# Five opening slots of an attention and MLP kernel with another order of work, other memsets, and one bank pool

## The chip, the cores and the metric

The kernel runs on one core of one Trainium2 chip. The metric is the device time of one execution in microseconds (us). The engines are TensorE (PE, with its weight loads shown as PEld), VectorE (DVE), ScalarE (ACT), GpSimd (POOL) and SyncE (SP). SP and POOL also issue DMAs from their queues. The inputs are drawn with a fixed seed.

## The reference

Attention with a forget gate for 8 batches of 8 heads, 576 positions, head size 64, and an MLP behind it:

```python
scores = scale * np.matmul(q, k.transpose(0, 1, 3, 2))
log_f = np.log(np.clip(f, 0.0001, 1.0))
cum = np.cumsum(log_f, axis=-1)
decay = cum[:, :, :, None] - cum[:, :, None, :]
scores = np.where(causal, -1000000000.0, scores + decay)
attn = softmax(scores)                       # over the last axis, with 1e-09 added to the sum
x = (attn @ v) in rows of 8 * 64             # 4608 rows of 512
h = x @ w_in                                 # 512 -> 2048
out = (h - np.tanh(h)) @ w_out               # 2048 -> 512
```

## The kernel before

The attention works on pairs of heads: 8 batches of 4 pairs, `pairs[p]`. A slot p holds the scores of pair p and the values of pair p - 1, so that PE does not wait for the exponentials of the pair in hand. In all but the first five slots, steps of the MLP stand between the attention's pieces. All engines follow the order in which the program emits the instructions (`tc.manual_schedule`), so each engine's queue is the order of the calls in the code. An instruction that waits holds up all that stands behind it on its engine.

**Loads.** q, k, v and the weights come by DMAs that POOL issues, and are cast to 16 bits on the way. `load_qk` brings some heads of q or k in rows of positions (`qn`, `kn`), `load_v_head`, `load_v_block` and `load_v_rest` bring v (`vn`), `load_win` a quarter of the first weight (512 of 2048 columns, which are four of the 16 tiles `ft`), `load_wout` a half of the second. Those of batches 0 and 1 and of the weights are emitted in one run before the slots. SP issues the loads of f, small rows (`const_rows`, `load_aug`), transposes from batch 1 on, and the output.

**Preparation.** VectorE clears constants and pads by memsets, clamps f, and after ACT's logarithm does the running sum (`tensor_tensor_scan`) and splits it into two 16-bit rows `chi` and `clo` (in `cc`). These are added to the scores either as extra rows of `QT`/`KT` or, for the first head, by extra matmuls (`direct` in `scores`) with `pick` as selector. `pick[:, 2:3]`, which the second head needs for tile 4 alone, is written in `pads()`.

**Pieces of a slot.** The lists `FIRST[p]` spell slots 0 to 4:

- a number: that many matmuls on constants (`spin`).
- `q`n, `k`n: `trans` for pair p + n. PE turns the head pair's q or k by six transposes into a bank from `t_bank`, and VectorE copies the bank into `QT` or `KT` in two instructions (ACT does it for the first q).
- `s`i: `scores` of tile i alone, and `g`i: of a group of tiles, (0, 1), (2, 4), (5, 6) or (3). Tiles 0 to 2 are the first head's, 4 to 6 the second's, 3 the last key block of both. ACT then takes the exponential of the bank or of both banks (L358). Tile 3 uses a bank of `t_bank` in slots 0 to 3.
- `va`, `vb`: `values` of the pair before, first and second head, 15 matmuls each, into one pair of banks `av` that exists once. After `vb` VectorE forms the reciprocal sums `rs` and divides, `xn` (L385 to L387).
- `y`, `x`: `turn` of the pair two before or one before. PE transposes `xn`, VectorE copies it into `XR`, the input of the MLP.
- `p`, `r`, `c`: `pads()`, `later_rows()`, and rows of constants.
- `h`, `m`: the first MLP matmuls of `mlp1` without their last quarter, and one step of the list `mlp`.

`t_bank` gives in slots 0 to 3 two banks in turn, `t2` and `tr`, afterwards `tr` alone. In slot 0 single tiles of scores go to four banks (`ps_one`), in slots 1 to 3 pairs of banks come from a pool of two (`ps_two`), which takes over the same memory. From slot 4 on there are three banks for the MLP and two for scores.

From slot 5 on `att_items` gives the order, with `trans` of the next pair behind given tiles, and the MLP steps are spread between the items. Each unit u of 512 rows runs 16 steps `mlp1`, one for each tile `ft` in the order `turns`: four matmuls, ACT's tanh, and VectorE's sum (`gt`). Where a pair of tiles and its partner are done, `sums` adds them for the second product, which follows in 14 steps (`product`, a scheme with seven instead of eight block products). Sums of the weight's blocks (`wsum`) stand at steps 14 to 23 of the first unit.

Of the kernel before, what the change touches and what calls it, by code (L numbers as in the profile page):

```python
# [14 lines left out]
PITCH = 640  # L15
VW = 66
SHIFT = 5.0
FAR = 3
BIG = 32768.0


@with_exitstack
def kernel(
# [63 lines left out]
    def load_qk(dst, src, b, h0, h1):  # L87
        nc.gpsimd.dma_start(
            out=dst[b % 2][:, h0:h1, :, :].rearrange("p h n d -> p (h n) d"),
            in_=src[b, h0:h1, :, :].rearrange("h s d -> (h s) d").rearrange("(m p) d -> p m d", p=S // NT6))  # L90
# [51 lines left out]
    def load_aug(b, h0=0):  # L142
# [3 lines left out]
        nc.sync.dma_start(out=KT[i][D + 1:D + 2, h0:H, 0:S], in_=cc[NH + b * H + h0:NH + b * H + H, :])  # L146

    nc.vector.memset(id16, 0.0)
    nc.vector.memset(ones16, 1.0)
    nc.gpsimd.affine_select(out=id16, in_=id16, compare_op=ALU.not_equal,  # L150
                            fill=1.0, base=0, pattern=[[-1, P]], channel_multiplier=1)
    load_qk(qn, q, 0, 2, 4)
    load_qk(kn, k, 0, 2, 4)
    nc.vector.memset(minus16, -1.0)
    const_rows(0, 1, H)
    nc.vector.memset(pick, 0.0)
    nc.vector.memset(pick[0:1, 0:1], -1.0)
# [1 line left out]
    nc.vector.memset(pick[0:1, 1:2], 1.0)  # L159
    nc.vector.memset(cqs[NH:P, :], 0.0)  # L160
    nc.vector.memset(KT[0][D:D + 3, 0, :], 0.0)
    nc.vector.tensor_scalar(out=lf, in0=lf, scalar1=0.0001, scalar2=1.0,
                            op0=ALU.max, op1=ALU.min)
    nc.vector.memset(neg16, 0.0)
    nc.vector.memset(tri16, 0.0)
    nc.vector.memset(QT[0][D:D + 3, 0, :], 0.0)
    load_qk(qn, q, 0, 4, 6)
    load_qk(kn, k, 0, 4, 6)
    nc.gpsimd.affine_select(out=neg16, in_=neg16, compare_op=ALU.not_equal,
# [16 lines left out]
    load_v_head(0, 1)  # L186
    load_v_rest(0)
    load_qk(qn, q, 0, 6, H)
    for n in range(NJ - 1):
        load_v_block(0, n, 2, H)  # L190
    load_qk(kn, k, 0, 6, H)

    def pads():
        nc.vector.scalar_tensor_tensor(out=pick[:, 2:3], in0=id16[:, 1:2], scalar=-1.0, in1=id16[:, NH + 1:NH + 2],
                                       op0=ALU.mult, op1=ALU.subtract)
        for e in EL:
            nc.vector.memset(e, 0.0)
        nc.vector.memset(KT[0][0:D, :, S:PITCH], 0.0)
        nc.vector.memset(KT[0][D:D + 3, 1:H, S:PITCH], 0.0)
        nc.vector.memset(vn[0][D:P, NJ - 1, :, :], 0.0)  # L200
        nc.vector.memset(vn[0][:, :, :, D:VW], 1.0)

    def later_rows():
        nc.vector.memset(KT[1][:, :, S:PITCH], 0.0)
        nc.vector.memset(vn[1][D:P, NJ - 1, :, :], 0.0)
        nc.vector.memset(vn[1][:, :, :, D:VW], 1.0)
        const_rows(1, 0, H)
        load_aug(1)

# [9 lines left out]
    for h0, h1, then in ((0, 2, (0, 2)), (2, 4, ("v", 1)), (4, 6, (3,)), (6, H, ())):  # L219
        load_qk(qn, q, 1, h0, h1)  # L220
        load_qk(kn, k, 1, h0, h1)
        for i in then:
            if i == "v":
                load_v(1)
            else:
                load_win(i * QW, (i + 1) * QW)
# [90 lines left out]
    def scores(b, c, tis, how):  # L317
        n2 = len(tis)
        if "t" in POOLS and tis[0] == LAST:
            banks = t_bank().rearrange("p (o w) -> p o w", o=1)  # L320
        else:
            banks = POOLS["s"].tile([P, 2 if how == "group" else 1, UW], FP32, tag="sc", name="ps")
        if tis[0] == LAST:
            eb = EL[(b * NPAIR + c) % 3].rearrange("p (o w) -> p o w", o=1)
        else:
            g, o = PLACE[tis[0]]
            if b == 0:
                if o == 0:
                    EB[(b, c, g)] = gtp.tile([P, 2, UW], FP16, tag="gt", name="e2")
                eb = EB[(b, c, g)][:, o:o + n2, :]  # L330
            else:
                eb = aex.tile([P, 1, UW], FP16, tag="e", name="e")
        for i, ti in enumerate(tis):
            ps, e = banks[:, i, :], eb[:, i, :]
            for a, j, i0, n, col in TILES[ti]:
                h = 2 * c + a
                edge = min(P, n) if how != "late" and i0 == j * P else 0
                direct = b == 0 and (h == 0 or h == 1 and ti == 4)
                minus, plus = (pick[:, 0:1], pick[:, 1:2]) if h == 0 else (pick[:, 2:3], id16[:, 1:2])
                kn_ = min(P, S - j * P) if direct else P  # L340
                rows = D if direct and h else D + 3
                nc.tensor.matmul(out=ps[:, col:col + n], lhsT=KT[b % 2][0:rows, h, j * P:(j + 1) * P],  # L342
                                 rhs=QT[b % 2][0:rows, h, i0:i0 + n], start=True, stop=not (edge or direct))
                if direct:
                    nc.tensor.matmul(out=ps[0:kn_, col:col + n], lhsT=cc[:, j * P:j * P + kn_],
                                     rhs=minus.to_broadcast([P, n]), start=False, stop=False)
                    nc.tensor.matmul(out=ps[:, col:col + n], lhsT=plus.to_broadcast([P, P]),
                                     rhs=cqs[:, i0:i0 + n], start=False, stop=not edge)
                if edge:
                    nc.tensor.matmul(out=ps[:, col:col + edge], lhsT=neg16, rhs=tri16[:, 0:edge],  # L350
                                     start=False, stop=True)
                for ib in range(j, NJ):
                    w0 = min(ib * P, S - P)
                    if i0 <= ib * P < i0 + n:
                        E[(b, c, a, j, ib)] = e[:, col + w0 - i0:col + w0 - i0 + P]
        lo = min(x[4] for x in TILES[tis[0]])
        hi = max(x[4] + x[3] for x in TILES[tis[0]])
        nc.scalar.activation(out=eb[:, :, lo:hi], in_=banks[:, 0:n2, lo:hi], func=AF.Exp, scale=qscale)  # L358
        if how != "late":
            return  # L360
        ti, e = tis[0], eb[:, 0, :]
        col, cp, step, wd = MASKS[ti]
        view = e[:, col:col + (cp - 1) * step + wd]
        if cp == 1:
            pat = [[1, wd]]
        else:
            view = bass.AP(view.tensor, view.offset, [list(view.ap[0]), [step, cp], [1, wd]])
            pat = [[0, cp], [1, wd]]
        nc.gpsimd.affine_select(out=view, in_=view, compare_op=ALU.is_ge, fill=0.0,  # L369
                                base=0, pattern=pat, channel_multiplier=-1)  # L370
# [127 lines left out]
    turns = [o + 2 * i + e for i in range(K2 // 2) for o in (0, K2) for e in range(2)]  # L498
    mlp = []
    for u in range(NU):  # L500
        mlp += [[(mlp1, u, ft)] for ft in turns]
        mlp += [[(product, u, n, g)] for n, g in ((1, 0), (1, 1), (2, 0), (6, 0), (6, 1), (2, 1))]
        mlp += [[(product, u, n, g)] for n in (5, 7, 3, 4) for g in range(2)]
    for at, n in ((NFT - 2, 0), (NFT, 2), (NFT + 3, 1), (NFT + 6, 3)):
# [5 lines left out]
    def step():  # L510
        for fn, *args in mlp[STEPS[0]]:
            fn(*args)
        STEPS[0] += 1

    FIRST = [["8", "q0", "2", "k0", "3", "s0", "s1", "q1", "s2", "k1", "p", "s4", "s5", "q2", "s6", "s3"],
# [4 lines left out]

    def first_slot(p):
        here = pairs[p]
# [32 lines left out]
    def att_items(p):  # L555
        items = []
        before = pairs[p - 1]
        after = pairs[p + 1] if p + 1 < len(pairs) else None
        for ti in range(len(TILES)):
            if p < len(pairs):  # L560
                items.append((lambda ti=ti: scores(*pairs[p], (ti,), "late"), True))
            items += [(load, False) for load in LOADS.get((p, ti), ())]
            if after and after[0] < FAR and ti in ((1, 4) if p == 2 * NPAIR - 1 else (3, 5) if p == NPAIR + 1 else (0, 3)):
                dst, src = (KT, kn) if ti > 3 or ti == 3 and p != NPAIR + 1 else (QT, qn)
                items.append((lambda dst=dst, src=src: trans(*after, src, dst, "AA" if 2 * NPAIR - 1 <= p <= 2 * NPAIR else "VV"), True))
            if ti == 1:
                items += [(lambda a=a: values(*before, a), a == 1) for a in range(2)]
                items.append((lambda: turn(*before), True))
        return items

    with tc.manual_schedule(engines={PE, mybir.EngineType.Pool, mybir.EngineType.SP, mybir.EngineType.DVE,
                                     mybir.EngineType.Activation}):
        with tc.tile_pool(name="ps_t2", bufs=1, space=PSUM) as POOLS["t"]:
            with tc.tile_pool(name="ps_one", bufs=4, space=PSUM) as POOLS["s"]:
                first_slot(0)
            with tc.tile_pool(name="ps_two", bufs=2, space=PSUM) as POOLS["s"]:
                POOLS["s"].tile([P, 2, UW], FP32, tag="sc", name="ps")
                for p in range(1, NPAIR):
                    first_slot(p)
        del POOLS["t"]  # L580
        POOLS["m"] = ctx.enter_context(tc.tile_pool(name="ps_m", bufs=3, space=PSUM))
# [42 lines left out]
```

## Time and profile before

| | us |
|---|---|
| median of three runs | 352.36 |
| the three runs | 352.36, 348.66, 882.66 |
| the profiled execution | 347.94 |
| its span, first to last instruction | 346.2 |
| matmuls of PE in the span, busy | 333.2 |
| VectorE, busy | 253.6 |
| ACT, busy | 219.7 |
| POOL, busy | 177.6 |

Busy time of PE is modelled from starts, so a busy PE is not one at its peak. An idle stretch is put down to the engine or load whose signal came last. "Issue to landing" of a load counts from the start of the instruction on POOL that issues it.

### The profile page before, as it was taken

The numbers are of one execution on the slowest core, as the hardware profiler recorded it, in microseconds if no ns is written. First come the engines' busy times: TensorE is split into PE (matmuls) and PEld (weight loads), VectorE is DVE, ScalarE is ACT, GpSimd is POOL, SyncE is SP. The second block draws the span as 40 slices with busy tenths as digits, with TensorE's granted clock in tenths as the row PEclk, the third lists the DMA queues.
The fourth block names the chain that finished last, engine by engine and source line by source line (L and its number), as shares of the span: only waits on it lengthen the run. The fifth ranks groups of instructions, "written<-read, shape, count | busy, mean of one in ns | idle before, by whom it ended". The sixth has DMA issues, their size and how long they took to land.

```text
span 346.2 us, 8657 instructions
## 1 busy us (share of the span) xinstructions
PE 333.2 (96%) x3297; PEld 234.0 (68%) x3297; DVE 253.6 (73%) x524; ACT 219.7 (63%) x412; POOL 177.6 (51%) x324
## 2 busy tenths in 40 slices
PE   8878979999999999999999999999999999999996
PEld 3666547875578557887886568756887786486475
DVE  7674989929994789658974898488838864873872
ACT  6663868867765786578656875687558843633631
POOL 8987258686677727773767357752222220500500
PEclk9998999999999999999999999999999999999999
DMA  9999999999999999999899969992221013003003
GB/s 99 131 169 170 185 200 147 130 137 165 135 133 135 159 137 97 114 185 145 84 110 163 175 76 114 180 164 43 58 92 27 19 45 112 0 17 107 3 0 123
DMA packets 169592, 38.82 MB, mean 112 GB/s; under 512 B 155938, under 2 KB 169486, under 8 KB 169550
## 3 DMA queue, kind: packets, MB, share of 16 engines
q0 software_dynamic: 116608, 18.36, 80.1%
q1 hardware_dynamic: 52942, 19.90, 28.8%
q8 instruction: 26, 0.43, 0.5%
q14 instruction: 16, 0.13, 0.1%
HBM read 36.85 MB, written 9.44 MB: 134 GB/s over the span
## 4 chain that ended last, share of the span: by engine, by line
PE 82%; DVE 10%; ACT 3%; DMA 2%; issue 1%; SPq 1%; DVEq 0%; ACTq 0%
PE mb L414 32%; PE px L462 16%; PE mb L462 13%; PE ps L342 12%; PE av L379 7%; DVE gt L427 2%; DVE sm L441 2%; DMA out_dram<-ost 2%; ACT e L358 1%; DVE ws L271 1%; DVE xn L387 1%; PE t L289 1%; DVE KT L299 1%; ACT th L421 1%; DMA ws<-in_f_dram 1%
## 5 line engine op out<-in xcount | busy, mean ns | idle before, releaser
L414 PE MATMUL mb<-XR,win 128*128 128x512 f16 (+4 forms) x704 | 141.2, 340 | 1.5 <-DVE gt L427 1.2
L358 ACT ACTIVATE e<-ps 128x512 f16<-128x512 f32 (+1 forms) x183 | 109.6, 618 | 26.2 <-PE ps L342 15.2
L421 ACT ACTIVATE th<-mb 128x512 f32<-128x512 f32 x144 | 86.5, 601 | 51.5 <-PE mb L414 45.9
L427 DVE TENSOR_TENSOR gt<-mb,th 128x512 f16<-128x512 f32 x144 | 97.3, 687 | 24.1 <-ACT th L421 23.1
L369 POOL TENSOR_SCALAR_AFFINE_SELECT e<-e 128x128 f16<-128x128 f16 x162 | 59.2, 368 | 102.0 <-ACT e L358 101.2
L414 PEld LDWEIGHTS <-win 128*128 128x128 f16 x704 | 61.8, 97 | 49.8 <-issue 3.4
L342 PE MATMUL ps<-QT,KT 67*128 67x448 f16 (+4 forms) x376 | 74.3, 280 | 2.0 <-ACT e L358 1.4
L462 PEld LDWEIGHTS <-gt 128*128 128x128 f16 x576 | 53.8, 97 | 10.8 <-DVE gt L427 1.0
L342 PEld LDWEIGHTS <-KT 67*128 67x128 f16 x384 | 36.7, 98 | 22.2 <-issue 2.5
L462 PEld LDWEIGHTS <-sm 128*128 128x128 f16 x432 | 40.4, 97 | 6.7 <-issue 0.4
L462 PE MATMUL mb<-ws,gt 128*128 128x256 f16 x288 | 36.4, 272 | 0.0
L379 PEld LDWEIGHTS <-e 128*128 128x128 f16 x896 | 32.7, 98 | 3.6 <-DVE xn L387 0.6
L379 PE MATMUL av<-vn,e 128*128 128x65 f16 x896 | 34.5, 194 | 0.4 <-DVE xn L387 0.4
L479 ACT ACTIVATE part<-px 128x512 f32<-128x512 f32 x24 | 14.3, 597 | 30.1 <-PE px L462 30.1
L492 DVE TENSOR_TENSOR ost<-mb,part 128x512 f32<-128x512 f32 x25 | 17.1, 685 | 21.5 <-PE mb L462 6.8
L462 PE MATMUL px<-ws,sm 128*128 128x256 f16 x256 | 31.6, 272 | 0.0
L113 POOL DMA_DIRECT2D vn<-in_v_dram x32 | 28.4, 902 | 1.8 <-issue 1.2
L387 DVE TENSOR_TENSOR xn<-av,rs 128x640 f16<-128x640 f32 x32 | 26.4, 825 | 1.1
L441 POOL TENSOR_TENSOR sm<-gt 128x512 f16<-128x512 f16 x4 | 4.6, 1156 | 36.3 <-DVE gt L427 36.3
L94 POOL DMA_DIRECT2D qn<-in_q_dram x25 | 21.9, 875 | 1.5 <-issue 1.4
L94 POOL DMA_DIRECT2D kn<-in_k_dram x25 | 21.4, 855 | 1.3 <-issue 1.1
L385 DVE TENSOR_SCALAR rs<-av 128x10 f32<-128x10 f32 x32 | 5.1, 160 | 23.0 <-PE av L379 22.9
(92 smaller groups left out, 321.6 us busy)
## 6 DMA issues: line engine op xcount, KB each, us to landing
out_dram<-ost SPq DMA_DIRECT2D x34, 256.0 KB
vn<-in_v_dram POOLq DMA_DIRECT2D x28, 128.0 KB, 5.6
qn<-in_q_dram POOLq DMA_DIRECT2D x20, 128.0 KB, 3.8
kn<-in_k_dram POOLq DMA_DIRECT2D x20, 128.0 KB, 4.4
win<-in_moe_w_in_dram POOLq DMA_DIRECT2D x4, 512.0 KB, 8.8
wout<-in_moe_w_out_dram POOLq DMA_DIRECT2D x2, 1024.0 KB, 16.1
qn<-in_q_dram POOLq DMA_DIRECT2D x10, 144.0 KB, 7.0
kn<-in_k_dram POOLq DMA_DIRECT2D x10, 144.0 KB, 6.8
```

What stands on the lines that cost most here:

```text
L94: nc.gpsimd.dma_start(out=dst[b % 2][0:pn, n, :].rearrange("p (h d) -> p h d", h=H), in_=src[b, :, n * P:n * P + pn, :].rearrange("h p d - ...
L113: nc.gpsimd.dma_start(out=vn[b % 2][:, n, h0:h1, 0:D], in_=v[b, h0:h1, n * P:(n + 1) * P, :].rearrange("h p d -> p h d"))
L342: nc.tensor.matmul(out=ps[:, col:col + n], lhsT=KT[b % 2][0:rows, h, j * P:(j + 1) * P], rhs=QT[b % 2][0:rows, h, i0:i0 + n], start=True, ...
L358: nc.scalar.activation(out=eb[:, :, lo:hi], in_=banks[:, 0:n2, lo:hi], func=AF.Exp, scale=qscale)
L369: nc.gpsimd.affine_select(out=view, in_=view, compare_op=ALU.is_ge, fill=0.0, base=0, pattern=pat, channel_multiplier=-1)
L379: nc.tensor.matmul(out=av[:, a, ib, :], lhsT=E.pop((b, c, a, j, ib)), rhs=vn[b % 2][:, j, 2 * c + a, 0:D + 1], start=(j == 0), stop=(j == ib))
L387: nc.vector.tensor_tensor(out=xn.rearrange("p i (a d) -> p a i d", a=2), in0=av[:, :, :, 0:D], in1=rs.to_broadcast([P, 2, NJ, D]), op=ALU. ...
L414: nc.tensor.matmul(out=hps[:, o:o + n], lhsT=win[:, ci, ft * P:(ft + 1) * P], rhs=XR[:, ci, t:t + n], start=(ci == 0), stop=(ci == NCH - 1))
L421: nc.scalar.activation(out=th, in_=hps, func=AF.Tanh, scale=-1.0)
L427: nc.vector.tensor_tensor(out=GT[(u, ft)], in0=hps, in1=th, op=ALU.add)
L462: nc.tensor.matmul(out=ps[:, g * E2:(g + 1) * E2], lhsT=left(k), rhs=right[:, k, :], start=(first and (g == 0 or last) and k == 0), stop=( ...
L492: nc.vector.tensor_tensor(out=ost, in0=ps, in1=PART.pop((u, {2: 1, 7: 5, 4: 6}[n])), op=ALU.add)
```

## The change

Seven things change, all in the preparation, in slots 0 to 5, in slot 9, and in the first unit's order of tiles:

1. `ones16` and `minus16` are written as 32-bit words.
2. VectorE clears `neg16` and `tri16` ahead of the clamp of f, and the pad columns of `KT[0]` ahead of the scan instead of in `pads()`.
3. The memsets of `KT[1]` and `vn[1]` go from VectorE in slot 1 to GpSimd (`later_pads`), in the queue of loads ahead of v of batch 1. The fourth quarter of k of batch 0 is loaded ahead of v's blocks instead of behind them.
4. `pads()` stands before the first scores instead of behind the second k.
5. Slots 0 to 3 share one pool of two pairs of banks. A single tile of slot 0 takes a pair and uses half of it.
6. The lists of slots 1 to 4 have another order, and q of pair 4 is turned in slot 3 instead of slot 2. From slot 5 on, q and k of the next pair are turned one tile sooner in slot 5 and one tile later in slot 9.
7. In the first unit, tiles 6 and 7 come before 12 and 13, which need the last quarter of `w_in`.

On the engines, PE, ACT and SP keep their instructions in number; VectorE's queue has three memsets fewer, POOL's three more.

```diff
-    nc.vector.memset(ones16, 1.0)
+    nc.vector.memset(ones16.bitcast(U32), 0x3C003C00)
...
-    nc.vector.memset(minus16, -1.0)
+    nc.vector.memset(minus16.bitcast(U32), 0xBC00BC00)
...
+    nc.vector.memset(neg16, 0.0)
+    nc.vector.memset(tri16, 0.0)
     nc.vector.tensor_scalar(out=lf, in0=lf, scalar1=0.0001, scalar2=1.0,
                             op0=ALU.max, op1=ALU.min)
-    nc.vector.memset(neg16, 0.0)
-    nc.vector.memset(tri16, 0.0)
     nc.vector.memset(QT[0][D:D + 3, 0, :], 0.0)
+    nc.vector.memset(KT[0][0:D, :, S:PITCH], 0.0)
...
     load_qk(qn, q, 0, 6, H)
+    load_qk(kn, k, 0, 6, H)
     for n in range(NJ - 1):
         load_v_block(0, n, 2, H)
-    load_qk(kn, k, 0, 6, H)
...
         for e in EL:
             nc.vector.memset(e, 0.0)
-        nc.vector.memset(KT[0][0:D, :, S:PITCH], 0.0)
...
+    def later_pads():
+        nc.gpsimd.memset(KT[1][:, :, S:PITCH], 0.0)
+        nc.gpsimd.memset(vn[1][D:P, NJ - 1, :, :], 0.0)
+        nc.gpsimd.memset(vn[1][:, :, :, D:VW], 1.0)
+
     def later_rows():
-        nc.vector.memset(KT[1][:, :, S:PITCH], 0.0)
-        nc.vector.memset(vn[1][D:P, NJ - 1, :, :], 0.0)
-        nc.vector.memset(vn[1][:, :, :, D:VW], 1.0)
...
             if i == "v":
+                later_pads()
                 load_v(1)
...
-            banks = POOLS["s"].tile([P, 2 if how == "group" else 1, UW], FP32, tag="sc", name="ps")
+            banks = POOLS["s"].tile([P, 2 if "t" in POOLS else 1, UW], FP32, tag="sc", name="ps")
...
-        mlp += [[(mlp1, u, ft)] for ft in turns]
+        mlp += [[(mlp1, u, ft)] for ft in (turns if u else turns[:10] + turns[12:14] + turns[10:12] + turns[14:])]
...
-    FIRST = [["8", "q0", "2", "k0", "3", "s0", "s1", "q1", "s2", "k1", "p", "s4", "s5", "q2", "s6", "s3"],
-             ["r", "g0", "g1", "k1", "va", "g2", "vb", "g3"],
-             ["g0", "q1", "va", "g1", "k1", "vb", "y", "g2", "g3", "q2"],
-             ["g0", "y", "k1", "va", "g1", "vb", "g2", "g3"],
-             ["c", "s0", "va", "y", "vb", "s1", "h0", "h1", "x", "h2", "q1", "s2", "m", ...]]
+    FIRST = [["8", "q0", "2", "k0", "3", "p", "s0", "s1", "q1", "s2", "k1", "s4", "s5", "q2", "s6", "s3"],
+             ["r", "k1", "g0", "g1", "va", "vb", "g3", "g2"],
+             ["g0", "q1", "g1", "y", "k1", "va", "vb", "g3", "g2"],
+             ["g0", "q1", "va", "g1", "k1", "vb", "y", "g3", "g2"],
+             ["c", "va", "y", "vb", "s0", "s1", "h0", "h1", "x", "h2", "q1", "s2", "m", ...]]
...
-            if after and after[0] < FAR and ti in ((1, 4) if p == 2 * NPAIR - 1 else (3, 5) if p == NPAIR + 1 else (0, 3)):
-                dst, src = (KT, kn) if ti > 3 or ti == 3 and p != NPAIR + 1 else (QT, qn)
+            if after and after[0] < FAR and ti in ((1, 4) if p in (2 * NPAIR - 1, 2 * NPAIR + 1) else (2, 4) if p == NPAIR + 1 else (0, 3)):
+                dst, src = (KT, kn) if ti > 2 else (QT, qn)
...
-            with tc.tile_pool(name="ps_one", bufs=4, space=PSUM) as POOLS["s"]:
-                first_slot(0)
             with tc.tile_pool(name="ps_two", bufs=2, space=PSUM) as POOLS["s"]:
-                POOLS["s"].tile([P, 2, UW], FP32, tag="sc", name="ps")
-                for p in range(1, NPAIR):
+                for p in range(NPAIR):
                     first_slot(p)
```

The lists of slot 4 are the same from "s2" on.

More of the change, by code (lines that the diff above doesn't have):

```diff
@@ L19 @@
 BIG = 32768.0
+U32 = mybir.dt.uint32
 @with_exitstack
```

2 rows, old and new, of the table FIRST are left out of this document.

## The prediction, made before the changed kernel ran

> **What bounds the kernel now.** I read the page first, then the busy time by stretches, then PE's waits, then the timeline of the first 50 us. The page:
>
> ```profile
> PE 333.2 (96%) x3297; PEld 234.0 (68%) x3297; DVE 253.6 (73%) x524; ACT 219.7 (63%) x412; POOL 177.6 (51%) x324
> ```
>
> The share hides stages. The windows view (stretch, length, then busy time and count of PE, PEld, DVE, ACT, POOL, granted clock, DMA share, GB/s):
>
> ```profile
> 21.00:24.40 3.40, 2.18 (x31) 1.56 (x28) 2.78 (x7) 1.70 (x4) 2.61 (x3) 1.00 1.21 195
> 24.40:27.80 3.40, 3.14 (x40) 2.78 (x41) 1.48 (x4) 1.24 (x2) 0.85 (x2) 0.52 1.99 164
> 27.80:31.20 3.40, 2.42 (x52) 2.07 (x50) 1.39 (x4) 2.35 (x4) 2.72 (x4) 0.98 2.38 158
> 40.00:50.00 10.00, 8.23 (x84) 4.80 (x83) 8.40 (x17) 6.32 (x13) 5.80 (x12) 1.00 1.31 201
> 50.00:60.00 10.00, 10.00 (x126) 6.96 (x125) 9.71 (x20) 8.23 (x16) 7.22 (x14) 1.00 2.51 156
> 200.00:300.00 100.00, 99.90 (x998) 71.37 (x997) 72.93 (x146) 64.33 (x123) 39.04 (x83) 1.00 0.58 80
> ```
>
> From 50 us on PE has no room, so whatever the first slots save moves the rest forward whole. PE's room lies in slots 0 to 5; no engine is full there, so its waits are handovers. The stretch with least PE work (2.18 of 3.40) is followed by one at clock 0.52, and 2.42 of 3.40 was followed by none.
>
> **Slot 0.** Timeline of before, first slots (start, duration, engine; in brackets the idle time before and its releaser):
>
> ```profile
> 1.07 0.54 DVE L149 MEMSET ones<- 128x576 f16 x1
> 2.35 0.30 DVE L160 MEMSET cqs<- 64x288 uint32 x1
> 4.85 1.35 DVE L176 TENSOR_TENSOR_SCAN ws<-ones,ws 64x576 f32<-64x576 f16 x1 [0.19 <-ACT ws L173]
> 8.18 0.39 PE L342 MATMUL ps<-QT,KT 67*128 67x512 f16 x1
> 10.08 0.92 DVE L299 COPY QT<-t 64x576 f16<-64x576 f16 x2 [1.30 <-PE t L289]
> 10.85 0.60 ACT L358 ACTIVATE e<-ps 128x512 f16<-128x512 f32 x1 [0.44 <-PE ps L350]
> 12.16 0.38 PE L345 MATMUL ps<-pick,cc 128*128 128x512 f16 x1 [0.76 <-DVE pick L194]
> 12.42 0.27 DVE L198 MEMSET KT<- 64x256 uint32 x1
> 13.41 0.12 DVE L201 MEMSET vn<- 128x80 f16 x1
> 14.47 0.38 PE L342 MATMUL ps<-QT,KT 67*128 67x512 f16 x1 [0.38 <-ACT e L358]
> 15.28 2.91 ACT L358 ACTIVATE e<-ps 128x1024 f16<-128x1024 f32 x3 [0.69 <-PE ps L342]
> ```
>
> *Memsets.* `ones16` and `minus16` as 32-bit words cost 0.30 each instead of 0.54, by the 288-word row. The first scores at 8.18 still hang on f's load, the clamp, Ln and the scan, which waits for ACT until 4.85; two memsets pass the clamp into idle time and KT's 0.27 fills the room before 4.85. Worth nothing at 8.18, and at most 0.1 late if that room is short. SP's rows of constants, which read both tiles, may go out 0.5 earlier on an unchanged queue, and nobody waits for them.
>
> *pads earlier.* From 12.1, when `pick` lets PE go, to the last pad's end at 13.53 are 1.4; less KT's 0.27 and its gap (0.3 to 0.4) that is 1.1, and with `pick`, one column, at the 0.12 of the smallest row, 1.2. They now run from 8.8 (10.08 - 1.30) to 10.0 or 10.1, in VectorE's idle time before q1's copy, so their cover is just enough. PE no longer waits 0.76 for pick; tile 4 ends at 11.8 instead of 12.8, since its three further products follow each 0.22, as tile 0's did.
>
> *Two banks instead of four.* Tile 6 must wait until ACT has read tile 4: 11.84 + 0.60 + a signal = 12.5 against 12.2, a wait of 0.3. Tiles 2, 4 and 5 find their bank read. q2's copy ends at 13.35, not 14.46.
>
> **Slots 1 to 4.** More of the timeline:
>
> ```profile
> 17.55 0.38 PE L342 MATMUL ps<-QT,KT 67*128 67x512 f16 x1
> 18.10 0.42 PE L289 MATMUL t<-id,qn 96*128 96x96 f16 x6
> 17.62 0.17 DVE L385 TENSOR_SCALAR rs<-av 128x10 f32<-128x10 f32 x1 [0.60 <-PE av L379]
> 18.07 0.82 DVE L387 TENSOR_TENSOR xn<-av,rs 128x640 f16<-128x640 f32 x1
> 23.14 0.41 PE L289 MATMUL t<-id,qn 96*128 96x96 f16 x6 [1.21 <-DVE XR L398]
> 23.39 0.38 PE L342 MATMUL ps<-QT,KT 67*128 67x512 f16 x1
> 32.85 0.44 PE L397 MATMUL t<-id,xn 128*128 128x128 f16 x5
> ```
>
> Two chain pieces give PE's short steps:
>
> ```profile
> 15.80 0.26 PE t L289 x6
> 16.05 0.46 PE av L379 x15
> ```
>
> With these I walk the new order by hand. The first scores pair takes 0.55 (17.55 to 18.10) for 1280 columns with its masks; by columns the two others (1408) take 0.6, tile 3 (256) 0.13 with its starts, a turn (640) 0.28. Six transposes take 0.27, half the values 0.46; ACT takes 0.97 a pair (2.91 / 3) and 0.28 for tile 3; VectorE takes 0.92 for a pair of copies, half of it for the one of a turn, and 1.28 from rs to the end of xn (17.62 to 18.89). Each result counts 0.15 after PE's last issue and 0.04 for the signal.
>
> Slot 1: k1 waits for q2's copy and starts at 13.35, g0 at 13.6 (before 14.47), g1 14.2, both values 14.8 to 15.7, g3, g2 to 16.45. ACT reads g2 by 17.64; xn is ready at 17.2 (before 18.89), sooner because both halves of the values stand together ahead of g2, and no memset of batch 1 or k1's copy stands between.
> Slot 2: g0 16.45 (17.55), q1, then g1 waits 0.4 for its bank until 17.68; y, k1, both values, g3, g2 to 20.5. The old 1.21 at 23.14, two turns of one bank behind xn, is gone.
> Slot 3: g0 20.5 (23.39), q1, then va waits 0.15 for xn, g1, k1, vb, y to 23.55; g3 waits 0.4 for k1's copy; g2 to 24.7.
> Slot 4: va waits 0.5 for the last xn until 25.25, y, vb, s0 at 26.45, s1, h0, h1, and x at 28.3 against 32.85: **4.5 us sooner**.
>
> Walked the same way, the old order puts x at 33.1 with matmuls at half clock from 24.5 to 27.9, and at 31.3 without. So about 1.8 of the gain is the clock: the new slots leave PE idle at most 0.6 in any 3.4 us, nearer the 2.42 row than the 2.18 row in what is left empty.
>
> The Trainium skill ("TensorE: Matmul & The Clock Gate", Part 1: The HAM clock gate) says the half clock comes after at least one idle window of about 3.4 us and that the windows run free of the kernel. The trace disagrees with the first half, since its stretch of 2.18 busy in 3.40 was enough. By the second, the drop may fall anywhere in a run.
>
> **Loads.** With 4.5 taken out, what arrives last? Answers for single loads (duration of the issue and its time, then issue to landing):
>
> ```profile
> L88 POOL DMA_DIRECT2D qn<-in_q_dram x1: 967/967/967, 18.3 to 18.3; - x1
> DMA to landing us min/median/max: 10.2/10.2/10.2
> L88 POOL DMA_DIRECT2D qn<-in_q_dram x1: 888/888/888, 28.7 to 28.7; - x1
> DMA to landing us min/median/max: 8.4/8.4/8.4
> L113 POOL DMA_DIRECT2D vn<-in_v_dram x4: 855/864/873, 10.9 to 13.4; - x4
> DMA to landing us min/median/max: 3.8/3.9/4.0
> ```
>
> Pair 5's q lands at 18.3 + 10.2 = 28.5 and slot 4 asks for it at 29.0 to 29.3. Pair 6's q lands at 28.75 + 8.4 = 37.1. v's last block landed at 17.2; with k's last quarter ahead of it, it is one issue (0.9 to 1.0) later, 18.2, and slot 2 asks at 18.8. All three just fit.
>
> GpSimd's three new memsets stand ahead of v, the second and fourth quarter of w_in, pairs 6 and 7 and w_out on POOL's queue. No row has such a write. The nearest:
>
> ```profile
> 59.14 0.51 POOL L369 TENSOR_SCALAR_AFFINE_SELECT e<-e 128x128 f16<-128x128 f16 x1
> 7.58 0.28 POOL L171 TENSOR_SCALAR_AFFINE_SELECT ws<-ws 128x128 f16<-128x128 f16 x1
> 24.74 0.70 POOL L105 DMA_DIRECT2D vn<-in_v_dram x1 [1.12 <-DMA win<-in_moe_w_in_dram]
> 27.65 0.76 POOL L211 DMA_DIRECT2D win<-in_moe_w_in_dram x1 [2.21 <-DMA win<-in_moe_w_in_dram]
> ```
>
> 512 + 528 + 80 elements a lane, at 0.28 to 0.51 for 128, are 2.5 to 4.5; if a fixed start is most of such a row, as little as 0.3 to 0.9. POOL idles 3.3 in the last two rows, waiting for transfers, so I take nothing, from 2.5 as the nearer row; without that cover up to 4.5 of lateness.
>
> The Trainium skill ("SBUF — State Buffer", Who interferes with whom) says a VectorE copy in a two-port mode and a GpSimd operation shut each other out for a whole instruction, which speaks against this move. No row here shows a GpSimd memset beside a copy.
>
> **Slot 5 and after.**
>
> ```profile
> 42.87 0.42 PE L289 MATMUL t<-id,qn 96*128 96x96 f16 x6
> 45.31 0.91 DVE L299 COPY QT<-t 64x576 f16<-64x576 f16 x2
> 46.36 0.41 PE L289 MATMUL t<-id,kn 96*128 96x96 f16 x6 [1.77 <-DVE QT L299]
> ```
>
> Pair 6's q turn moves ahead of one block of four matmuls (about 0.9), so it is wanted at 42.87 - 0.9 - 4.5 = 37.5, 0.4 after it lands. Its copy now precedes two sums, so k's turn loses most of the 1.77. VectorE is nearly full from 50 on, and the w_in order puts the third pair of sums two steps later, so little stays: 0.3, from -0.8 (two sums late) to +1.0 (what VectorE has idle, 1.6 in 40 to 50, less what its own waits keep). Slot 9's turns move by one tile each: within that.
>
> **Sum.** 4.5 + 0.3 = 4.8. The profiled execution took 347.94 (span 346.2 and 1.7 around it); 347.94 - 4.8 = **343.1 us**. The three runs before are 348.66, 352.36 and 882.66, so their median of 352.36 lies 1.3% over the execution that I argue from.
>
> **Rivals.**
> *The clock still drops.* The windows run free; a stretch as thin as 2.18 might still occur near 17 to 25. For it: four waits remain there. Against: they total 1.45 in 8 us. Only 4.8 - 1.8 = 3.0 is left: 344.9. Chance 0.17.
> *Loads hold slots 4 and 5.* Fits of 0.4 to 0.7 are thin; a landing 1 to 2 late costs as much once, 344.5 to 346. For: the queue is 10 us deep. Against: its order and bytes up to there are nearly the same. Chance 0.13.
> *GpSimd's writes make it slower.* If the memsets, shut out by copies, hold POOL for 4.5 or more and the idle 3.3 moves with them, pair 6's q lands later by that time and PE, in order, stands before its turn. Break-even is 4.9 + 0.4 = 5.3 of lateness; at 7 it is 347.94 + 1.7 = 349.6. Chance 0.08.
> *More comes back.* VectorE's idle time in slot 5 goes too and the first slots run without those four waits: 4.8 + 0.7 + 1.5 = 7.0, 340.9. Chance 0.1.
> *The order is not what binds.* ACT at 0.97 a pair, on two banks, paces slots 1 to 3: then only pick's 0.8 remains, 347.1. Slot 2's wait of 0.4 speaks for it, ACT's 1.70 busy in 3.40 against. Chance 0.04.
> The forecast keeps 0.48.
>
> **Numbers.** The range 340.3 to 348.0 leaves out the slower case (0.08), half of the best (0.05) and some scatter of runs. 2% is about what a measurement of this kernel can tell from no change: 341.0 by the profiled execution, but 345.3 by the median shown. If before repeats near 348 only the best case counts as faster (0.1); if its median stands, forecast, clock rival and best do (0.75). At 0.6 to 0.4: faster 0.36. Over 2% slower (354.9) needs 12 of lateness, and since no row bounds GpSimd's writes from above I leave it over half of its case: 0.05. The same: 0.59.
>
> **What would show it.** PE's wait for pick is gone and the pads end by 10.1; g0 of slots 1, 2, 3 near 13.6, 16.5, 20.5 and x near 28.3; no window at half clock between 20 and 32; POOL's memsets under 3.3 together, and q of pair 6 landing by 37.5; the 1.77 gone. I am wrong if a load or an ACT row stands as releaser ahead of PE in slots 2 to 5 for over 1 us.

## The result and the profile after

Time goes up a little: the ratio of after to before is 1.005, with a 95% interval of 1.003 to 1.007, which is 1.8 us. By the 2% bound it counts as the same. The medians of 20 runs each are 349.28 us (348.56 to 351.76) and 348.12 us (346.32 to 882.66), which is 1.2 apart. The ratio leaves out three slowed runs of before: 882.66, 353.13 and 352.36. The forecast was 343.1, its range ended at 348.0, so the time lies outside.

The profiled execution of after took 351.51 with a span of 349.7; before's took 347.94 with 346.2. After's lies 2.2 over its own median. Its mean granted clock was 0.99, as in 7 of the 20 runs; 12 had 0.994 or 0.995, and one had 1.0. So what follows shows where time is lost, and somewhat more of it than a common run loses.

The page of after, first part, PE's granted clock by slices, and the shares of the chain of waits by engine:

```profile
PE 334.1 (96%) x3297; PEld 233.6 (67%) x3297; DVE 253.0 (72%) x521; ACT 220.4 (63%) x412; POOL 179.3 (51%) x327
PEclk9999997899999999999999999999999999999999
PE 81%; DMA 8%; DVE 6%; ACT 2%; SPq 1%; issue 1%; POOL 0%; DVEq 0%; POOLq 0%
```

The engines' sums hardly differ. The dip to 7 and 8 lies in the seventh and eighth slice, 52 to 70 us, far behind the first slots. PE's waits (line, releaser, us in total, times, longest) name what is there:

```profile
PE t L293 <- DMA qn<-in_q_dram: 4.4, 2, 4.1
PE mb L418 <- DVE gt L431: 2.2, 3, 1.5
PE ps L346 <- DVE KT L303: 1.9, 3, 0.7
PE ps L346 <- DMA QT<-cqs: 0.6, 1, 0.6
PE av L383 <- DVE xn L391: 0.4, 1, 0.4
PE ps L346 <- ACT e L362: 0.3, 1, 0.3
```

One wait of 4.1 is for a load of q. The windows of after (columns as in the prediction):

```profile
21.00:24.40 3.40, 3.40 (x65) 2.86 (x63) 2.60 (x8) 2.89 (x4) 3.36 (x6) 1.00 1.13 172
24.40:27.80 3.40, 2.72 (x53) 2.08 (x51) 2.64 (x7) 1.65 (x3) 1.11 (x2) 1.00 1.86 177
40.00:50.00 10.00, 9.55 (x91) 5.21 (x90) 9.13 (x19) 7.65 (x16) 5.92 (x13) 1.00 1.35 200
50.00:60.00 10.00, 5.93 (x63) 4.55 (x62) 7.00 (x14) 5.08 (x10) 5.62 (x10) 0.83 2.87 145
60.00:70.00 10.00, 9.95 (x105) 7.84 (x103) 7.14 (x15) 6.55 (x12) 5.42 (x10) 0.83 2.65 133
```

Up to 50 us the plan works in this execution: 21 to 24.4 is full where it was 2.18 of 3.40, and no window is at half clock. Then comes a stretch that was 10.00 of 10.00 before and is 5.93 now. To see what each slot gains, the starts of the values of some pairs on PE, and the end, from the two traces:

```
values of pair     0      2      3      4      5      6      7      8      9     10     31    end
before         15.89  25.10  30.09  39.96  50.13  58.39  66.99  75.04  85.07  94.12 281.04 346.23
after          15.71  22.38  26.21  36.37  45.31  57.94  68.84  77.02  88.72  97.50 284.54 349.73
after earlier   0.18   2.72   3.88   3.59   4.82   0.45  -1.85  -1.98  -3.65  -3.38  -3.50  -3.50
```

4.8 us are gained by pair 5 and lost in three places: 4.4 ahead of pair 6, 2.3 ahead of pair 7, 1.7 ahead of pair 9. The timeline of after at the first place (in brackets the idle time and its releaser) and the load itself in the tile view (duration and time of the issue, who waited, issue to landing):

```profile
52.37 1.04 PE L466 MATMUL mb<-wout,gt 128*128 128x256 f16 x8
57.48 0.66 PE L293 MATMUL t<-id,qn 96*128 96x96 f16 x6 [4.07 <-DMA qn<-in_q_dram]
```

```profile
L89 POOL DMA_DIRECT2D qn<-in_q_dram x1: 891/891/891, 37.3 to 37.3; - x1
  PE t L293: 4.1, 1
DMA to landing us min/median/max: 20.1/20.1/20.1
```

The same load in before, and the turn that uses it:

```profile
L88 POOL DMA_DIRECT2D qn<-in_q_dram x1: 893/893/893, 40.9 to 40.9; - x1
DMA to landing us min/median/max: 13.0/13.0/13.0
58.13 0.42 PE L289 MATMUL t<-id,qn 96*128 96x96 f16 x6
```

This is q of pair 8, the first of batch 2, turned in slot 7. In before it lands at 40.9 + 13.0 = 53.9 and is asked for at 58.1: 4.2 us of slack. After asks 4.7 sooner, at 53.4 (57.48 - 4.07), and issues the load 3.6 sooner, but it lands 3.5 later, at 57.4. So the wait is the 4.7 that PE is ahead, less the 4.2 of slack, plus the 3.5 that the landing moved. Had the load landed at 53.9 again, PE would have waited only 0.5. Of the 3.5, 1.4 is that the second half of `w_out`, the load ahead of it, lands at 54.4 instead of 53.0 (34.9 + 19.5 and 34.3 + 18.7). The rest is that q of pair 8 follows 3.0 behind it instead of 0.9.

The second place follows from the first: the empty stretch is followed by two windows at half clock (56.7 to 63.5 by the records). The third is slot 9, timelines of before and after:

```profile
74.14 0.92 DVE L299 COPY QT<-t 64x576 f16<-64x576 f16 x2 [3.31 <-PE t L289]
77.70 0.69 DVE L492 TENSOR_TENSOR ost<-mb,part 128x512 f32<-128x512 f32 x1 [2.64 <-DMA out_dram<-ost]
```

```profile
79.48 0.69 DVE L496 TENSOR_TENSOR ost<-mb,part 128x512 f32<-128x512 f32 x1 [6.81 <-DMA out_dram<-ost]
80.09 0.91 DVE L303 COPY QT<-t 64x576 f16<-64x576 f16 x2
82.96 1.02 PE L418 MATMUL mb<-XR,win 128*128 128x512 f16 x4 [1.49 <-DVE gt L431]
```

With the turn one tile later, VectorE's copy of q (80.09) stands behind an output sum whose tile a DMA must first empty. The sum waits 6.81 with the copy behind it, and PE then waits 1.49 for VectorE's late `gt` and 0.7 for a `KT` copy.

### The profile page after: what moved, and what is told of

The parts are those of the page before. It is cut to its first block, busy times and chain, and to the rows that moved or that the text cites. A ratio compares the mean times of both kernels' runs of the same rounds, so it can differ in the third digit from the quotient of the medians.

```text
span 349.7 us, 8656 instructions
## 1 busy us (share of the span) xinstructions
PE 334.1 (96%) x3297; PEld 233.6 (67%) x3297; DVE 253.0 (72%) x521; ACT 220.4 (63%) x412; POOL 179.3 (51%) x327
## 4 chain that ended last, share of the span: by engine, by line
PE 81%; DMA 8%; DVE 6%; ACT 2%; SPq 1%; issue 1%; POOL 0%; DVEq 0%; POOLq 0%
PE mb L418 30%; PE px L466 16%; PE mb L466 14%; PE ps L346 11%; PE av L383 8%; DMA qn<-in_q_dram 6%; DMA out_dram<-ost 2%; DVE gt L431 1%; PE t L293 1%; DVE KT L303 1%; DMA ws<-in_f_dram 1%; ACT e L362 1%; DVE sm L445 1%; DVE xn L391 1%; ACT th L425 1%
## 5 line engine op out<-in xcount | busy, mean ns | idle before, releaser
L466 PEld LDWEIGHTS <-sm 128*128 128x128 f16 x432 | 40.9, 98 | 6.7
L383 PE MATMUL av<-vn,e 128*128 128x65 f16 x896 | 34.3, 194 | 0.4 <-DVE xn L391 0.4
L466 PE MATMUL mb<-wout,gt 128*128 128x256 f16 x160 | 22.2, 280 | 0.0
```

The source lines that it names most:

```text
L383: nc.tensor.matmul(out=av[:, a, ib, :], lhsT=E.pop((b, c, a, j, ib)), rhs=vn[b % 2][:, j, 2 * c + a, 0:D + 1], start=(j == 0), stop=(j == ib))
L466: nc.tensor.matmul(out=ps[:, g * E2:(g + 1) * E2], lhsT=left(k), rhs=right[:, k, :], start=(first and (g == 0 or last) and k == 0), stop=( ...
```

## The experiments

Kernels named a_ start from after, b_ from before. The letters of theories are those of the expectations; in words: (A) q of pair 8 has a bad place in POOL's queue, and the low clock follows from the wait; (B) the low clock comes by itself; (C) all loads run at the pace of one full stream, so that its place doesn't help; (D) loads issued behind it hold it up. Each line of results is the median, the number of runs, and the ratio to before with its 95% interval. Each group of kernels was timed beside its own runs of before, so a difference by ratios can differ from one by medians; where it matters both are given.

### Another place in the queue

a_early puts q and k of pair 8 between the two halves of `w_out`, b_early does the same to before. All three loads are then issued in slot 1.

```diff
-    for i in range(2):
-        load_wout(i * NFT // 2, (i + 1) * NFT // 2)
+    load_wout(0, NFT // 2)
+
+    def late_loads():
+        load_qk(qn, q, 2, 0, 2)
+        load_qk(kn, k, 2, 0, 2)
+        load_wout(NFT // 2, NFT)
...
                 later_rows()
+                late_loads()
```

> The changed kernel with one thing moved: the loads of q and k of pair 8 (first pair of batch 2) are issued ahead of the second half of w_out instead of from slot 5. Theory A (the load of pair 8's q is what PE waits for in slot 7, 4.1 us, and the two half-clock windows of about 3.0 us lost follow from that wait): the wait and the windows go, the time falls by 5 to 7 from 349.3, to 342.5 to 344.5. Theory B (the half clock comes of its own phase and the wait is incidental): the wait goes, the windows stay somewhere, 345 to 346. Theory C (the whole load stream binds, whatever its order): another load or w_out stands as releaser a few us away, and the time stays within 1 of 349.3.

> The kernel before, with the same two loads moved. There the q of pair 8 landed at 53.9 and PE asked at 58.1, so theory A expects no change beyond 0.7 us either way (348.1). If the order of the loads is worth something by itself, it is faster by more than 1.

a_early 347.89 (12), 1.0011 [0.998, 1.0043]; b_early 348.13 (12), 0.9991 [0.9964, 1.0017]. PE's waits in the first 100 us of a_early, and its timeline:

```profile
PE mb L470 <- DMA wout<-in_moe_w_out_dram: 2.1, 1, 2.1
PE t L297 <- DMA qn<-in_q_dram: 0.3, 1, 0.3
```

```profile
52.76 0.42 PE L297 MATMUL t<-id,qn 96*128 96x96 f16 x6
56.20 1.32 PE L470 MATMUL mb<-wout,gt 128*128 128x256 f16 x8 [2.11 <-DMA wout<-in_moe_w_out_dram]
```

The wait changes its name. q is there at 52.8, and PE now stands 2.1 us for the second half of `w_out`, which has moved behind it. 1.4 us come back, and not the 5 to 7 that a mere matter of place would give. The bytes that have landed of POOL's loads by 56 us, summed from the traces' packets, go with that: 8.32 MB in before, 8.07 in after, 8.19 in a_early (by 48 us 7.08, 6.89, 6.92). The place changes which load is late, and hardly how much has landed; an earlier PE finds no more bytes there.

### Loads behind it held back

a_hold, a_hold9 and a_hold_early issue v of batch 2 and the later q and k later, a_hold9 with slot 9's turns as in before, a_hold_early with the order of a_early. b_vearly is the reverse on before: v of batch 2 six places sooner (`10 + n`).

```diff
-    for o, (h0, h1) in ((8, (0, 2)), (10, (2, 4)), (21, (4, H))):
+    for o, (h0, h1) in ((8, (0, 2)), (21, (2, 4)), (24, (4, H))):
...
-            at_tile(p0, 16 + n if b == 2 else 7 + n + late, ...)
+            at_tile(p0, 23 + n if b == 2 else 7 + n + late, ...)
```

> The changed kernel with the loads that follow q and k of pair 8 (q and k of pair 9, v of batch 2, q and k of pairs 10 and 11) issued a slot later, in slot 7. In the runs so far pair 8's q landed the later the earlier it and these loads were issued (issued 40.9: 53.9; 40.6: 54.9; 37.3: 57.4). Theory D (loads in flight share the rate, so the loads behind hold up the one that PE waits for): q of pair 8 lands at 52 to 54.5, PE's wait of 4.1 falls under 1.2, no half clock in slot 7, and the time falls to 344 to 346. Theory C (the stream's bytes up to this load set its landing): it lands at 56.5 to 57.5 again and the time stays at 348.5 to 349.5.

> The first of these with slot 9's turns behind tiles 0 and 3 as before. If slot 9's later turns cost something of their own once slot 7 is on time, it is 0.5 to 1.5 faster than the first; if not, within 0.4 of it.

> The same, and q and k of pair 8 also ahead of the second half of w_out. Theory D: pair 8 lands before 50, w_out's second half 2 to 4 us sooner than the 56.2 of the run with the order alone, its wait of 2.1 falls under 0.5, 343 to 345. Theory C: w_out's second half lands near 56 again, 347.5 to 348.5.

> The kernel before with v of batch 2 issued six tiles sooner, near 47 instead of 53.6, while pair 8's q is still on its way. Theory D: q of pair 8 lands 1.5 to 3.5 later than 53.9, and as PE asks at 58.1 the time stays within 0.7 of before. Theory C: it lands at 53.5 to 54.5 as before.

a_hold 352.71 (11), 1.0117 [1.0083, 1.0152]; a_hold9 351.57 (12), 1.0097 [1.0064, 1.0129]; a_hold_early 350.94 (12), 1.0065 [1.0035, 1.0095]; b_vearly 348.08 (10), 1.0006 [0.9975, 1.0037]. The load in a_hold, by the tile view:

```profile
L89 POOL DMA_DIRECT2D qn<-in_q_dram x1: 893/893/893, 37.2 to 37.2; - x1
  PE t L293: 3.7, 1
DMA to landing us min/median/max: 19.6/19.6/19.6
```

With the loads behind it moved far back, it still lands 19.6 us after its issue, at 56.8 instead of 57.4. The loads behind it explain at most 0.6 of its lateness, and the theory that they hold it up falls. All three kernels are slower than after, which neither theory expected. In a_hold's trace PE waits for no other load up to 200 us, but 1.2 in all for GpSimd's masks; why holding the loads costs so much was not shown. In b_vearly q is issued at 39.3 instead of 40.9 and lands at 54.2 instead of 53.9: in before, too, an earlier issue buys no earlier landing.

Over the traces an earlier issue even goes with a later landing. With v of batch 1 loaded and pair 8 behind `w_out`, q issued at 36.6 to 37.5 landed at 56.3 to 57.4 (after, a_slot9, a_hold, a_hold9, a_late8); issued at 39.3 to 40.9 it landed at 53.9 to 55.7 (before, b_vearly, b_late8, a_spin, a_late89, a_late89_turns). The last three have after's loads in after's order, so the bytes ahead cannot be all that sets the landing. What else does stays open.

### Fewer bytes ahead of it

a_no_v1 and b_no_v1 replace the 576 KB of `load_v(1)` (0.56 MB in the expectations) by a GpSimd memset, b_no_v1b by two that spare the pads. Batch 1's values are then left out (zero).

```diff
-                load_v(1)
+                nc.gpsimd.memset(vn[1][:, :, :, 0:D], 0.0)
```

> The changed kernel without the five loads of v of batch 1, 0.56 MB of the stream ahead of pair 8's q; GpSimd clears that part of vn instead, so batch 1's values are left out (zero). Holding back the loads behind did not bring pair 8's q forward (56.8 and 56.3), nor did its place in the order help the time much, so theory C stands: the bytes up to this point set its landing. Theory C: the landing comes 2.5 to 4.5 sooner, the wait of 4.1 falls under 1.5, the half clock in slot 7 goes, and the time falls to 343.5 to 346.5. Theory B or another: PE waits in slot 7 as before and the time stays within 1 of 349.3.

> The kernel before without the same loads (batch 1's values left out). Theory C: no load held PE up there, so the time stays within 0.7 of 348.1. If shorter loads help by themselves, it falls as much as in the changed kernel.

> The kernel before without the loads of v of batch 1, as in the run before, but with GpSimd clearing only the part of vn that those loads fill, so that VectorE's memset of the rest doesn't wait for it (it did there, 7.7 us, which made that run useless as a control). Batch 1's values are left out (zero). Theory C: no load held PE up in the kernel before, so 347.4 to 348.8. If fewer loads help by themselves: 345 or less.

a_no_v1 345.13 (6), 0.9909 [0.9879, 0.9939]; b_no_v1 354.99 (6), 1.0188 [1.0157, 1.0219]; b_no_v1b 347.31 (12), 0.9976 [0.9953, 0.9999]. In a_no_v1, the load and the turn:

```profile
L89 POOL DMA_DIRECT2D qn<-in_q_dram x1: 884/884/884, 36.8 to 36.8; - x1
DMA to landing us min/median/max: 14.4/14.4/14.4
52.65 0.42 PE L293 MATMUL t<-id,qn 96*128 96x96 f16 x6
```

With 576 KB less ahead of it, q lands 6.2 us sooner than in after, at 51.2. At the 199 GB/s of 40 to 52 us those bytes alone are 3.0 by estimate, and the expectation had 2.5 to 4.5; in before leaving them out brings 3.8 (53.9 to 50.1). PE asks at 52.65 and waits for nothing, and no window is at half clock. Leaving v out brings before only 0.9 by median (348.24 to 347.31 in b_no_v1b), and brings after 4.2. So some 3.2 us of after's time are the stream's and what follows from its wait; by ratios they are 4.1.

b_no_v1 was meant as the control and is none, being slower for another reason. VectorE's and PE's waits in its first 40 us:

```profile
DVE vn L205 <- POOL vn L224: 7.7, 1, 7.7
PE ps L342 <- DVE KT L299: 6.2, 1, 6.2
```

VectorE's memset of the pad stood behind the new memset on GpSimd, in the order of writes to one tile, and held up the copy of `KT` behind it. b_no_v1b clears only what the pads' memsets don't touch.

### The clock

a_spin puts 20 matmuls on constants ahead of q's turn in slot 7, to keep PE busy while it would wait.

```diff
+                if p == 2 * NPAIR - 1 and ti == 1:
+                    items.append((lambda: spin(20), False))
```

> The changed kernel with 20 matmuls on constants ahead of pair 8's q turn in slot 7 (some 4.3 us at full clock), so that PE is busy while the load comes. Theory A with a clock that follows PE's idle time: the load still lands near 57.4, but the half-clock windows behind it go, and 2.5 to 3 of the 349.3 come back: 346.3 to 346.8. If the windows have nothing to do with the wait, they stay, and the time is 349.3 to 350.

348.88 (12), 1.0026 [0.9997, 1.0056]. 11 of 12 runs have the full clock, against 1 of 20 of after, so the empty stretch is what takes the clock away. But only 0.4 comes back by median (0.9 by ratio) where 2.5 to 3 were expected. After's own runs agree, as far as a single run at full clock can tell, that the clock is the smaller part: the one at full clock took 348.93, the median of the 12 at 0.994 or 0.995 is 349.25, that of the 7 at 0.99 is 350.64.

The profiled execution of a_spin can't show what PE waits for in those 11 runs, as it is the twelfth: 352.25, with half clock in slots 1 and 2 (14.6 to 21.4). PE came to the spins only at 56.5, when q had landed (54.9). Its row of tile 5 in slot 0, and two windows:

```profile
12.80 0.35 PE L346 MATMUL ps<-QT,KT 67*128 67x448 f16 x1 [0.84 <-ACT e L362]
11.20:14.60 3.40, 2.20 (x23) 1.33 (x23) 1.70 (x4) 2.14 (x5) 3.40 (x5) 1.00 1.91 127
14.60:18.00 3.40, 3.40 (x30) 2.48 (x31) 0.91 (x2) 1.55 (x3) 3.40 (x5) 0.50 2.03 133
```

So the first slots can still lose the clock. Tile 5 waits for ACT to read its bank, PE is busy 2.20 of 3.40, and half clock follows. Of the twelve traces with the new slots (after and all a_ kernels), five have this wait, 0.84 to 1.13 (a_spin, a_hold_early, a_no_v1_9, a_late89, a_late89_turns), and all but a_hold_early of these five then run at half clock from 14.6 to 15.6 on for 3.4 or 6.8 us.

### Slot 9

a_slot9 gives slot 9 alone its old turns.

```diff
-   ... ti in ((1, 4) if p in (2 * NPAIR - 1, 2 * NPAIR + 1) else ...
+   ... ti in ((1, 4) if p == 2 * NPAIR - 1 else ...
```

> The changed kernel with slot 9's turns behind tiles 0 and 3 again, as before. VectorE's copy of q stands there ahead of the second output sum, which waits for an output DMA, instead of behind it. If the 1.5 us wait of PE for gt at 83 comes from that, the time falls by 0.5 to 1.5, to 348 to 348.8. If slot 9 is only late because of slot 7, no change within 0.4.

349.02 (12), 1.0017 [0.999, 1.0043]: 0.26 less than after by median and 1.2 by ratio, which by itself decides nothing. Its trace shows the mechanism: PE's wait for `gt` is 0.50 instead of 1.49. a_no_v1_9 makes the same edit in a_no_v1, where no load hides it.

> The changed kernel without the loads of v of batch 1 (batch 1's values left out), and with slot 9's turns as before. It was 345.1 with slot 9 as changed, and PE still waited 1.5 and 0.7 there. If slot 9's turns cost that much: 343.3 to 344.2, near the 4.8 us that the first slots gain. If slot 9 is worth nothing: 344.8 to 345.5.

344.42 (12), 0.9902 [0.9871, 0.9932]; that is 0.7 less than a_no_v1 by median, 0.2 by ratio, and between the two expectations. In the profiled executions, the values of pair 8 to those of pair 9 take 11.65 in a_no_v1, 9.85 in a_no_v1_9 and 9.74 in b_no_v1b. The four pairs of kernels that differ in slot 9's turns alone have the same sign by median: 0.3, 0.7, 1.1 (a_hold, a_hold9) and 2.0 (a_late8 and a_late89, below). Only the last is clear of the scatter of its runs, so slot 9's cost is shown in kind, and in size only roughly.

### The turns of slot 7 later

Instead of bringing the load sooner, PE can ask later: a_late8 turns pair 8 behind tiles 3 and 5, a_late89 also gives slot 9 its old turns, a_late89_turns also undoes the first unit's order of tiles, and b_late8 is the control on before.

```diff
-   ... ti in ((1, 4) if p in (2 * NPAIR - 1, 2 * NPAIR + 1) else ...
-                dst, src = (KT, kn) if ti > 2 else (QT, qn)
+   ... ti in ((3, 5) if p == 2 * NPAIR - 1 else ...
+                dst, src = (KT, kn) if ti > (3 if p == 2 * NPAIR - 1 else 2) else (QT, qn)
```

> The changed kernel with all loads, and slot 7's turns of pair 8 behind tiles 3 and 5 instead of 1 and 4. PE asks for pair 8's q some 2.3 us later and does other work until then. Theory C: the wait falls from 4.1 to 1.5 to 2.2, less or no half clock, 346 to 347.5. If the turns' place binds in slot 8 (k's copy by ACT just ahead of the first scores), a new wait of 0.5 to 1.5 there takes part of it back: 347.5 to 348.5.

> The same with slot 9's turns behind tiles 0 and 3. In the changed kernel's trace PE waits 1.5 and 0.7 there where before it waited 0.3 and 0.5, so 0.5 to 1.4 less than the run with slot 7 alone: 345 to 347.

> The changed kernel with slot 7's turns behind tiles 3 and 5 and slot 9's as before (347.3), and the first unit's tiles in the old order. If the new order crowds VectorE's sums behind step 13 (waits for gt and for the weight's sums of 0.8 and 0.9 in that trace): 346.0 to 346.9. If it is worth nothing: within 0.4 of 347.3. If the old order waits for the last quarter of w_in again: 347.8 to 349.

> The kernel before with slot 7's turns behind tiles 3 and 5. Theory C: nothing was waited for there, so no gain: 347.8 to 349. If the later turns are an improvement by themselves: 346 to 347.3, and then the run of the changed kernel with them owes its gain to that.

a_late8 349.32 (12), 1.0019 [0.9988, 1.005]; a_late89 347.33 (12), 0.9969 [0.9941, 0.9996]; a_late89_turns 347.37 (12), 0.9966 [0.9935, 0.9997]; b_late8 348.35 (12), 0.9994 [0.9971, 1.0016]. PE's waits of a_late8 from 40 to 110 us:

```profile
PE av L383 <- POOL e L373: 2.2, 1, 2.2
PE mb L418 <- DVE gt L431: 1.5, 1, 1.5
```

The wait for q is gone in both, but a_late8 has 2.2 on GpSimd's masks instead, and slot 9's 1.5; it missed what was expected. The masks are late by the same stream. GpSimd issues the loads of v of batch 2 between them, and one of these issues stands behind the landing of `w_out`, with the next masks behind it:

```profile
54.94 0.89 POOL L114 DMA_DIRECT2D vn<-in_v_dram  x1 [2.51 <-DMA wout<-in_moe_w_out_dram]
```

In a_late89's trace no wait of PE from 40 to 110 us is over 0.6, and GpSimd does not wait for `w_out`. But this is an execution with half clock from 15.1 to 18.5, in which PE reaches pair 5's values 2.1 later than in after; its 7 runs at full clock (median 346.65) have no trace. With a_late89_turns it is the fastest full version found, 0.3% under before with an interval that just leaves 1 out, and needs the change: b_late8 shows nothing. The order of the first unit's tiles is worth nothing that can be seen. a_late89 is still 2.9 us over a_no_v1_9, 0.9 of which leaving v out gives before as well. Where the other 2 stay was not traced.

## Why the prediction was wrong

**The first slots were right in the profiled execution.** The timeline of after:

```profile
12.49 0.35 PE L346 MATMUL ps<-QT,KT 67*128 67x448 f16 x1 [0.55 <-DMA QT<-cqs]
14.54 0.38 PE L346 MATMUL ps<-QT,KT 67*128 67x512 f16 x1
18.64 0.30 PE L346 MATMUL ps<-QT,KT 67*128 67x320 f16 x1 [0.29 <-ACT e L362]
21.44 0.38 PE L346 MATMUL ps<-QT,KT 67*128 67x512 f16 x1
29.26 0.44 PE L401 MATMUL t<-id,xn 128*128 128x128 f16 x5
38.36 0.42 PE L293 MATMUL t<-id,qn 96*128 96x96 f16 x6
40.71 0.41 PE L293 MATMUL t<-id,kn 96*128 96x96 f16 x6
```

The pads end at 9.95, and the wait for `pick` is gone. The first scores of slots 1 and 3 start at 14.54 and 21.44, each about 0.9 after the forecast, and x at 29.26 instead of 28.3. One cause is the 0.55 at the top: tile 5 waits for a row of `cqs` that SP loads, a wait that the prediction does not have; of SP's other rows, those of constants, it says that nobody waits for them. In five other traces the same tile waits 0.84 to 1.13 for its bank, where the prediction has "Tiles 2, 4 and 5 find their bank read". The waits for a bank in slot 2 and for xn in slot 4 were 0.29 and 0.40, against 0.4 and 0.5. Slot 5's 1.77 is gone, as the two last rows show. At pair 5 the gain is 4.8, as the sum had it, but in part by luck: x gained less (3.6 instead of 4.5) and slot 5 more (1.2 instead of 0.3).

**GpSimd's memsets** were sized from masks of 128 elements, and are far smaller:

```profile
19.99 0.61 POOL L205 MEMSET KT<- 67x512 f16 x1
20.66 0.53 POOL L206 MEMSET vn<- 64x528 f16 x1
22.07 0.17 POOL L207 MEMSET vn<- 128x80 f16 x1
```

1.3 us in all, not 2.5. The rival in which they hold POOL up for 4.5 or more did not occur: the loads behind them are issued later than in before, but by 0.7 to 1.1 (`w_out` at 34.06 instead of 33.40), and q of pair 6 lands at 37.3 instead of 37.1. (The rival's break-even of 4.9 + 0.4 uses 4.9 where the sum has 4.8.) The first memset ran beside VectorE's copy of `KT` (20.10 to 21.01) and still took 0.61. Whether that copy is of the kind that the rule quoted in the prediction means (the Trainium skill, "SBUF — State Buffer", Who interferes with whom) is not shown, so this neither bears the rule out nor speaks against it.

**The step that failed** is "Loads. With 4.5 taken out, what arrives last?", with the sentence under the windows that carried it on: "From 50 us on PE has no room, so whatever the first slots save moves the rest forward whole." It went wrong twice. The list of arrivals stopped at pair 6, though a saving of 4.8 moves every later request forward by 4.8. The first load of batch 2, issued in slot 5 of before with 4.2 us of slack, is in the same trace and was left out; this alone would have cost 0.5. And the landings were taken from before as fixed. In after this load landed 3.5 later, at 57.4, and PE waited 4.1 for it in slot 7; a_no_v1, in which it lands at 51.2, has neither the wait nor the loss. So the loads are a bound of their own, which does not move forward with PE. Why the landing moved back is open beyond the 1.4 that the load ahead of it was late. The signs that would have shown the prediction wrong reached only to slot 5. The rival "Loads hold slots 4 and 5" had the mechanism, but two slots too early and at 1 to 2 us instead of 4.1.

**Two terms were mis-sized.** "Slot 9's turns move by one tile each: within that" costs 0.7 by the medians of a_no_v1 and a_no_v1_9 (0.2 by ratios). And the 1.8 for the clock was taken from a window that before's profiled execution had and most runs of before have not. The 127 runs of before beside the experiments, grouped by their granted clock:

```
granted clock   runs   median us
1.0               71      347.55
0.995             41      348.91
0.99 or less      15      351.68
```

One window of 3.4 us at half clock takes 3.4 x 0.5 / 348 = 0.005 off the mean clock, and a run with one is 1.4 us longer. Most runs had none to lose, so the slots' gain in them is near 3: a_no_v1_9 against b_no_v1b is 2.9 by median (344.42, 347.31), 3.2 by the runs at full clock (344.13, 347.31), 2.6 by ratios. That is the 3.0 of the rival "The clock still drops", though for another reason: the old slots mostly keep the clock. Its own mechanism occurred as well, as a_spin's windows show, near 11 to 15 us and not at 17 to 25. The "at most 0.6" of idle time in any 3.4 us of the new slots was too low: in after's trace 11 to 14.4 has 0.9, and a_spin's 11.2 to 14.6 has 1.2.

**The sum by medians**: -2.9 from the first slots where loads don't hold them, +0.7 for slot 9's turns, +3.2 for the stream's wait and the clock behind it: +1.0, beside the measured 1.2. By ratios it is -2.6 + 0.2 + 4.1 = +1.7, beside 1.8. Either closes by construction, since the terms are differences of a row of kernels; that each has its own kernel and its own line in a trace is what stands behind it. How the stream's term splits into wait and clock is not settled: a_spin puts the clock at 0.4 to 0.9, but spins of 4.5 us stand in its way.

## What to carry to other kernels

When a change makes an early stage faster, list every load with its landing and the time it is asked for, until the slack exceeds the saving; a load with less slack takes back part of the gain. The old landings are no promise for the new kernel: here one moved by 3.5 us the wrong way. Where the loads ran without a gap, another order mostly changed which one was late, and fewer bytes ahead or a later request took the wait away. Before a low clock in one profile goes into a sum, see how many of the runs have it; and before a variant's trace is read against another's, see whether both executions had the same clock.

## What the runs showed of the hardware

From 40 to 52 us the transfers kept one pace though PE had more to do in after. The windows of before and of after (last column GB/s):

```profile
40.00:52.00 12.00, 10.23 (x120) 6.22 (x119) 10.32 (x21) 7.40 (x15) 6.31 (x13) 1.00 1.34 199
```

```profile
40.00:52.00 12.00, 11.55 (x105) 6.55 (x104) 11.05 (x23) 9.65 (x20) 7.91 (x15) 1.00 1.35 199
```

PE is 1.3 us busier in after and 199 GB/s are moved in both. From 50 to 60 it was 156 and 145.

An issue that returns in 0.9 us says nothing of the landing, which came 13.0, 14.4 and 20.1 us later for the same kind of load.

A wait of PE of 4.07 us was followed by half clock in after's trace, and 19 of its 20 runs were granted less than the full clock, against 1 of 12 where spins fill the wait. Stretches with PE busy 2.00 to 2.20 of 3.40 were followed by half clock in before, a_spin, a_no_v1_9, a_late89 and a_late89_turns, but one of 2.18 (a_hold_early, 11.2 to 14.6) was not. Of before's 127 runs, at most 56 had a half-clock window after the thin stretch at 21 us.
